# A two-layer transformer kernel on one core: adds moved from TensorE to VectorE, attention weights spread by two DMAs, and the order of the steps rearranged

## Chip, cores and metric

The kernel runs on one core of a Trainium2 chip. The metric is the device time of one execution in microseconds (us); medians are of three to seven runs. All runs quoted here were fast (none is over 0.5% above the fastest run of its kernel). A ratio is the mean time of one kernel's fast runs over that of the other's of the same rounds, so it is not quite the ratio of the medians that stand beside it. The profile is one execution, and its span is 1.7 to 1.8 us shorter than the time of that same run.

Names: PE is TensorE, DVE is VectorE, ACT is ScalarE, POOL is GpSimd; SP issues the weight loads. "oT" is the attention output that the output projection Wo reads; "abc" holds the attention weights, spread over 128 partitions; "a" is the softmax result from which abc is made; "tmp" is the DVE instruction that frees an accumulator of the second feed-forward GEMM.

## The reference, cut to what matters

```python
# B=1, S=2048, D=1024, F=3584, 32 heads of 32; windows of 8 positions, dilation 2
def _A_ref(x, wqkv, wo):                 # local attention
    q, k, v = ...                        # x @ wqkv
    kg, vg = k[..., idx_c, :], v[..., idx_c, :]      # 8 earlier positions: s, s-2, ... s-14
    logits = einsum("bhsd,bhswd->bhsw", q, kg) * scale     # masked at the start of the sequence
    o = einsum("bhsw,bhswd->bhsd", softmax(logits), vg)
    return o @ wo
def _B_ref(x, w1, b1, w2, b2):           # feed-forward
    return gelu(x @ w1 + b1) @ w2 + b2
x = x + _A_ref(layernorm(x), A_wqkv, A_wo);  x = x + _B_ref(layernorm(x), B_w1, B_b1, B_w2, B_b2)
x = x + _A_ref(layernorm(x), A_wqkv, A_wo);  x = x + _B_ref(layernorm(x), B_w1, B_b1, B_w2, B_b2)
```

## The kernel before

The sequence is cut into four groups of 512 tokens. Two layers times four groups make eight steps, n = 0 to 7. A step is: q, k, v projections (24 chunks of 8 matmuls), attention, Wo (8 chunks), first GEMM (28 units of 8 matmuls), second GEMM (32 units of 7). PE works in the program's order: its timeline of one middle step of the kernel before shows Wo (394.73 us), the projections (407.90) with the head sum among them (458.37), the first GEMM and then the second (498.64). DVE work of the next step is laid beside PE work of this one by hand: `stage(gen, count, sides)` runs a generator of PE units and calls the side functions at the given units.

The attention of one step has four parts. DVE makes q·k products for 8 chunks; a matmul with a 0/1 matrix sums them over a head into PSUM (L, a "head sum", one group of 8 matmuls). `attend` is the softmax. `spread` copies each head's weights to four partitions, by writing them to DRAM and reading them back, or by matmul. `av` multiplies with v and sums (4.3 us of DVE per chunk, eight chunks).

```python
def spread(n, on_pe=False):
    ...
    if on_pe:                                     # steps 0, 1 and 7
        ... 8 matmuls with selbc and 8 ACT copies; return
    a_d = dram.tile([H, W, T], BF16, name="a_d")
    for tb in range(NTT):                         # 4 DMAs out
        pool.dma_start(a_d[:, :, tb * P:(tb + 1) * P], a[tb * H:(tb + 1) * H, :, :])
    for j in range(HP):                           # 4 DMAs in
        pool.dma_start(abc[j::HP, :, :], a_d[:, :, :])

def gen_ffn2(n):
    for dh in range(2):
        pss = [acc_tile() for _ in range(NTT)]    # 4 of the 6 accumulators
        for kq in range(4):
            ... load one weight tile
            for tt in range(NTT):
                ... 7 matmuls
                if kq == 3:                       # the accumulator is freed by DVE
                    vec.tensor_tensor(out=tmp[:], in0=pss[tt][:], in1=b2bc[...], op=ALU.add)
                    vec.tensor_tensor(out=xs, in0=tmp[:], in1=xs, op=ALU.add)
                yield

# the schedule of most steps
for n in range(2, N - 1):
    stage(gen_wo(n))
    stage(gen_qkv(n + 1))
    last = n + 2 == N
    stage(gen_ffn1(n), sides=at(4, attend, n + 1) + at(9 if last else 4, spread, n + 1, last) + each(av, n + 1, 9, 2))
    ...
```

## Time and profile before

| | before |
|---|---|
| time, median of 3 | 1281.39 us (1280.09 to 1281.58) |
| span of the profile | 1278.2 us |
| PE busy / DVE busy | 1252.9 / 808.3 us |
| GEMM matmuls | 5632, 215.9 ns apart when nothing interrupts |

First part of the page of the kernel before: busy time, share of the span, instructions.

```profile
PE 1252.9 (98%) x5861; PEld 630.7 (49%) x5910; DVE 808.3 (63%) x843; ACT 322.4 (25%) x502; POOL 85.0 (7%) x217
```

The waits view of PE before: what PE waited for, us in total, times, longest.

```profile
PE L L115 <- DVE big L93: 3.7, 6, 2.5
PE acc L115 <- DMA wt<-in_A_wo_dram: 3.3, 1, 3.3
PE acc L115 <- ACT abc L93: 2.7, 2, 2.4
PE acc L115 <- DVE x_91 L93: 2.3, 1, 2.3
...
```

PE is the bottleneck, and it hardly waits. 5632 x 215.9 ns is 1216 us, so all else that PE does or waits for is 62 us: that is all that a change of schedule can win.

The DMA part of the page (count, KB each, median us from issue to landing):

```profile
abc<-a_d POOLq DMA_DIRECT2D x20, 256.0 KB, 4.2
a_d<-a POOLq DMA_DIRECT2D x20, 64.0 KB, 2.1
```

The four DMAs out were issued in 2.35 us and had landed 2.18 us later. From the end of a to the first v product took 10.8 us here.

### The profile page before, as it was taken

To read this page: it belongs to the slowest core of one execution; us is meant where nothing else is said; L and a number is where in the kernel's file an instruction comes from. 1 tells how busy PE (TensorE), PEld (TensorE's weight loads), DVE (VectorE), ACT (ScalarE), POOL (GpSimd) and SP (SyncE) were. 2 spreads that over 40 slices of the span, in tenths; PEclk is the share of its full clock that TensorE was granted. 3 is DMA by queue.
4 is the path that set the end of the run, shared out by engine and by line. 5 is a ranking of instruction groups with operands and counts; after the bars stand their busy time and mean duration, and the time that the engine had idled before them with its cause. 6 is when DMAs were issued, how large, how long until landed. Compare 5 with 4: busy or idle time off the path is not lost.

```text
span 1278.2 us, 14116 instructions
## 1 busy us (share of the span) xinstructions
PE 1252.9 (98%) x5861; PEld 630.7 (49%) x5910; DVE 808.3 (63%) x843; ACT 322.4 (25%) x502; POOL 85.0 (7%) x217
## 2 busy tenths in 40 slices
PE   9989899999999999999999999999999999999998
PEld 5546454444445644456444554446544464444443
DVE  4877489977317769279583696837875557942003
ACT  4353243102300342013510235002440035300410
POOL 4010000020000020000200002000030000000000
PEclk9989999999999999999999999999999999999999
DMA  8663364385546465555556655565566564466441
GB/s 280 190 164 132 132 174 151 108 238 178 160 153 181 147 202 160 177 162 176 185 161 187 187 164 178 164 203 156 185 186 187 177 196 132 146 175 202 140 144 51
DMA packets 216352, 216.42 MB, mean 169 GB/s; under 512 B 67808, under 2 KB 186592, under 8 KB 213600
## 3 DMA queue, kind: packets, MB, share of 16 engines
q1 hardware_dynamic: 214528, 208.69, 54.4%
q0 software_dynamic: 1760, 6.83, 1.7%
q8 instruction: 46, 0.75, 0.2%
q14 instruction: 18, 0.15, 0.0%
HBM read 194.26 MB, written 5.51 MB: 156 GB/s over the span
## 4 chain that ended last, share of the span: by engine, by line
PE 75%; DVE 18%; issue 2%; ACT 2%; DMA 2%; SPq 0%; POOL 0%; DVEq 0%; ACTq 0%; POOLq 0%
PE acc L115 74%; DVE big L93 17%; DMA x_91<-in_A_x_dram 1%; PE L L115 1%; ACT abc L93 1%; ACT xn L93 0%; DVE z L93 0%; DVE stats L93 0%; DMA wt<-in_A_wo_dram 0%; DMA xnT<-xn 0%; SPq L93 0%; ACT kT L93 0%; ACT qT L93 0%; DVE oT L93 0%; DVE a L93 0%
## 5 line engine op out<-in xcount | busy, mean ns | idle before, releaser
L115 PE MATMUL acc<-xnT,wt 128*128 128x512 bf16 x3328 | 728.3, 381 | 3.0 <-ACT abc L93 2.4
L115 PEld LDWEIGHTS <-wt 128*128 128x128 bf16 x3328 | 395.3, 119 | 334.3 <-issue 17.4
L115 PE MATMUL acc<-wt,hT 128*128 128x512 bf16 x1752 | 386.5, 379 | 2.1
L115 PEld LDWEIGHTS <-hT 128*128 128x128 bf16 x1792 | 175.2, 98 | 211.7 <-issue 0.4
L93 ACT ACTIVATE hT<-acc,b1T 128x512 bf16<-128x512 f32 x224 | 152.7, 687 | 266.4 <-PE acc L115 265.7
L93 DVE TENSOR_TENSOR tmp<-acc,b2bc 128x512 f32<-128x512 f32 x64 | 44.2, 690 | 271.8 <-PE acc L115 269.0
L93 DVE TENSOR_TENSOR big<-big 128x1024 bf16<-128x1024 bf16 (+2 forms) x170 | 209.9, 1279 | 1.2
L93 DVE TENSOR_TENSOR big<-qT,kT 128x4096 bf16<-128x4096 bf16 x64 | 143.6, 2286 | 63.7 <-ACT kT L93 54.4
L93 DVE TENSOR_TENSOR big<-abc,vT 128x4096 bf16<-128x4096 bf16 x64 | 143.5, 2282 | 22.3 <-ACT abc L93 15.3
L93 ACT CAST qT<-acc 128x512 bf16<-128x512 f32 x64 | 37.0, 585 | 373.7 <-PE acc L115 373.7
L115 PE MATMUL acc<-wt,oT 128*128 128x512 bf16 x503 | 115.0, 387 | 6.2 <-DMA wt<-in_A_wo_dram 3.3
L115 PEld LDWEIGHTS <-oT 128*128 128x128 bf16 x512 | 50.8, 99 | 69.0 <-issue 11.2
L93 POOL TENSOR_TENSOR rstd<-mv,eps_t 128x1 f32<-128x1 f32 x64 | 12.8, 201 | 792.0 <-DVE mv L93 791.1
L93 ACT CAST kT<-acc 128x512 bf16<-128x512 f32 x64 | 37.3, 587 | 78.0 <-PE acc L115 78.0
L93 ACT CAST vT<-acc 128x512 bf16<-128x512 f32 x64 | 37.6, 588 | 76.2 <-PE acc L115 76.2
L93 POOL TENSOR_TENSOR rstd<-rstd,mhalf 128x1 f32<-128x1 f32 x64 | 38.4, 601 | 5.0
L93 POOL DMA_DIRECT2D a_d<-a x20 | 11.8, 615 | 235.6 <-DVE a L93 235.6
L93 ACT ACT_TABLE_LOAD x14 | 18.0, 1283 | 35.1 <-PE acc L115 34.1
L93 DVE TENSOR_REDUCE z<-e 128x128 f32<-128x1024 f32 x8 | 15.3, 1915 | 13.8 <-ACT e L93 13.8
L93 DVE TENSOR_TENSOR oT<-big 128x512 bf16<-128x512 bf16 x64 | 24.0, 413 | 0.0
L93 ACT ACTIVATE e<-e 128x1024 f32<-128x1024 f32 x8 | 8.5, 1058 | 34.8 <-DVE e L93 34.7
L115 PE MATMUL L<-big,smat 128*32 128x512 bf16 x176 | 13.2, 384 | 3.7 <-DVE big L93 3.7
(116 smaller groups left out, 336.8 us busy)
## 6 DMA issues: line engine op xcount, KB each, us to landing
wt<-in_B_w_dram SPq DMA_DIRECT2D x56, 1024.0 KB, 5.5
wt<-in_B_w_dram SPq DMA_DIRECT2D x64, 896.0 KB, 4.9
wt<-in_A_wqkv_dram SPq DMA_DIRECT2D x48, 1024.0 KB, 5.5
wt<-in_A_wo_dram SPq DMA_DIRECT2D x16, 1024.0 KB, 5.0
abc<-a_d POOLq DMA_DIRECT2D x20, 256.0 KB, 4.2
a_d<-a POOLq DMA_DIRECT2D x20, 64.0 KB, 2.1
xnT<-xn SPq DMA_TRANSPOSE x60, 5.0
x_87<-in_A_x_dram SPq DMA_DIRECT2D x1, 256.0 KB, 2.7
```

The costliest lines, as they stand in the source:

```text
L93: inst = f(*args, **kwargs)
L115: return pe(nc.tensor.matmul(*args, **kwargs))
```

## The change

Its intent is to take work from PE and to remove PE's few waits:

- In steps 0 and 1 DVE adds the chunk products, so two head sums per step are left of eight (12 more DVE adds of 2.29 us).
- All spreads go by DMA (none by matmul), and by two DMAs rather than eight.
- The layernorms of groups 1 and 2 come before the first products and are normalized by DVE.
- The v weights of some steps are loaded later. Wo of steps 1 and 7 stands after 6 units of the second GEMM, not 4; products of steps 1, 2 and 7 are split around other work; attention of the middle steps starts at unit 7, not 4; that of step 2 at unit 12 of the first GEMM of step 1.

```diff
-    def head_sum(n, prod, last):
+    def head_sum(n, last=True):
...
-        if s["on_pe"]:
-            if len(tree) > 2:
-                head_sum(n, tree.pop(0), False)
-        elif c % 2 == 1:
-            for _ in range(min(2, len(tree) - 1)):
+        if c % 2 == 1:
+            for _ in range(1 if c % (NCH // s["parts"]) == 1 else 2):
                 b = tree.pop()
                 vec.tensor_tensor(out=tree[-1][:], in0=tree[-1][:], in1=b[:], op=ALU.add)
...
-        for tb in range(NTT):
-            pool.dma_start(a_d[:, :, tb * P:(tb + 1) * P], a[tb * H:(tb + 1) * H, :, :])
-        for j in range(HP):
-            pool.dma_start(abc[j::HP, :, :], a_d[:, :, :])
+        pool.dma_start(a_d[:].rearrange("h w (b t) -> b h w t", b=NTT), a[:])
+        src = a_d[:]
+        pool.dma_start(abc[:], bass.AP(tensor=src.tensor, offset=src.offset, ap=[[W * T, H], [0, HP], [1, W * T]]))
...
+        stage(gen_qkv(0, 2), sides=at(0, ln_a, 1) + at(2, load_x, 2) + at(4, ln_a, 2, early) + ... + at(18, head_sum, 0, False))
+        stage(q1, sides=at(3, attend, 0) + at(3, spread, 0) + each(new_prod, 1, 8, 1, 0, 4) + each(av, 0, 12, 1))
...
-    stage(f2, 4)
+    stage(f2, 6)
     stage(gen_wo(1))
...
+    stage(gen_ffn1(1), sides=at(0, hold) + each(new_prod, 2, 0, 1, 4, 8) + at(12, attend, 2) + at(12, spread, 2) + each(av, 2, 13, 2))
...
-        stage(gen_ffn1(n), sides=at(4, attend, n + 1) + at(9 if last else 4, spread, n + 1, last) + each(av, n + 1, 9, 2))
+        stage(gen_ffn1(n), sides=at(7, attend, n + 1) + at(7, spread, n + 1) + each(av, n + 1, 9, 2))
...
+    q = gen_qkv(n + 1, defer=True, v_late=True)          # n = 6
+    stage(q, 16, sides=each(new_prod, n + 1, 8, 1, 0, 4))
+    stage(gen_wo(n))
+    stage(q, sides=each(new_prod, n + 1, 0, 1, 4, 8))
+    stage(gen_ffn1(n), sides=at(3, attend, n + 1) + at(3, spread, n + 1) + each(av, n + 1, 4, 2))
+    f2 = gen_ffn2(n)
+    stage(f2, 6)
+    stage(gen_wo(n + 1))
+    stage(f2)
```

The DMA out: its DRAM side has dimensions 4 (token blocks) x 32 (heads) x 8 x 128, so the outermost one counts 4.

More of the change, by code (lines that the diff above doesn't have):

```diff
@@ L75 @@
     smp = ctx.enter_context(tc.tile_pool(name="smp", bufs=1))
-    iop = ctx.enter_context(tc.tile_pool(name="iop", bufs=2))
+    iop = ctx.enter_context(tc.tile_pool(name="iop", bufs=1))
     psum = ctx.enter_context(tc.tile_pool(name="psum", bufs=1, space=PSUM))
@@ L135 @@
     smat = const.tile([P, H], BF16, name="smat")
-    selbc = const.tile([P, P], BF16, name="selbc")
     maskrow = const.tile([1, W, 16], BF16, name="maskrow")
@@ L156, in build_constants @@
         pool.memset(onesrow[:], 1.0)
-        pool.memset(selbc[:], 1.0)
-        for tb in range(NTT):
-            sb = selbc[tb * H:(tb + 1) * H, :]
-            pool.affine_select(out=sb, in_=sb, pattern=[[1, P]], compare_op=ALU.is_ge, fill=0.0, base=0, channel_multiplier=-HP)
-            pool.affine_select(out=sb, in_=sb, pattern=[[-1, P]], compare_op=ALU.is_ge, fill=0.0, base=HP - 1, channel_multiplier=HP)
     def load_bias():
@@ L179, in ln_stats, with ln_norm, ln_tile @@
         return mv, rstd
-    def ln_norm(t, mv, rstd, on_act=False):
-        xn = lnp.tile([P, D], BF16, name="xn")
-        if on_act:
-            nmr = lnp.tile([P, 1], F32, name="nmr")
-            pool.tensor_tensor(out=nmr[:], in0=mv[:, 0:1], in1=rstd[:], op=ALU.mult)
-            pool.tensor_scalar(out=nmr[:], in0=nmr[:], scalar1=-1.0, scalar2=None, op0=ALU.mult)
-            act.activation(xn[:], x[t][:], ACT.Identity, bias=nmr[:], scale=rstd[:])
-        else:
-            vec.tensor_scalar(out=xn[:], in0=x[t][:], scalar1=mv[:, 0:1], scalar2=rstd[:], op0=ALU.subtract, op1=ALU.mult)
+    def ln_norm(t, mv, rstd):
+        xn = lnp.tile([P, D], BF16, name="xn", bufs=3)
+        vec.tensor_scalar(out=xn[:], in0=x[t][:], scalar1=mv[:, 0:1], scalar2=rstd[:], op0=ALU.subtract, op1=ALU.mult)
         return xn
-    def ln_tile(t, tt, xnT, on_act=False):
+    def ln_tile(t, tt, xnT):
         mv, rstd = ln_stats(t)
-        xn = ln_norm(t, mv, rstd, on_act)
+        xn = ln_norm(t, mv, rstd)
         sp.dma_start_transpose(xnT[:, tt, :, :], xn[:].rearrange("s (k p) -> s k p", p=P))
@@ L211, in ln_first, with new_xnT @@
         vec.on = False
-    def new_xnT():
-        return xnp.tile([P, NTT, KD, P], BF16, name="xnT")
+    def new_xnT(pool=None):
+        return (pool or xnp).tile([P, NTT, KD, P], BF16, name="xnT")
     def win(t_ap):
@@ L238, in qkv_chunk @@
         return ps
-    def head_sum(n, prod, last):
-        first = "L" not in st[n]
-        if first:
+    def head_sum(n, last=True):
+        if "L" not in st[n]:
             st[n]["L"] = psum.tile([P, W, P], F32, name="L", bufs=1)
+            start = True
+        else:
+            start = False
         L = st[n]["L"]
+        first = n % NG == 0
+        prod = st[n]["prods"].pop(0)
         for wh in range(2):
@@ L247, in head_sum @@
                 mm(L[tb * H:(tb + 1) * H, wh * 4:(wh + 1) * 4, :], lhsT=smat[:],
-                   rhs=prod[:, wh * 4:(wh + 1) * 4, tb * P:(tb + 1) * P],
-                   start=first, stop=last, skip_group_check=True, tile_position=(0, tb * H))
+                   rhs=prod[:, wh * 4:(wh + 1) * 4, tb * P:(tb + 1) * P], start=start,
+                   stop=last and not (first and tb == 0), skip_group_check=True, tile_position=(0, tb * H))
+        if first and last:
+            for w in range(W - 1):
+                mm(L[0:H, w, 0:HALO], lhsT=onesrow[:], rhs=maskrow[0:1, w, 0:HALO], start=False, stop=True,
+                   skip_group_check=True, tile_position=(0, 0))
     def new_prod(n, c):
@@ L257, in new_prod, with gen_qkv @@
         tree.append(prod)
-        if s["on_pe"]:
-            if len(tree) > 2:
-                head_sum(n, tree.pop(0), False)
-        elif c % 2 == 1:
-            for _ in range(min(2, len(tree) - 1)):
+        if c % 2 == 1:
+            for _ in range(1 if c % (NCH // s["parts"]) == 1 else 2):
                 b = tree.pop()
                 vec.tensor_tensor(out=tree[-1][:], in0=tree[-1][:], in1=b[:], op=ALU.add)
-    def gen_qkv(n, sum_on_pe=False, defer=False, qk_pool=None):
+    def gen_qkv(n, parts=1, defer=False, qk_pool=None, v_late=False):
         g = n % NG
@@ L269, in gen_qkv @@
         s = st[n]
-        s["on_pe"] = sum_on_pe
+        s["parts"] = parts
         s["prods"] = []
@@ L282, in gen_qkv @@
             yield
-        wv = load_qkv(2)
+        if not v_late:
+            wv = load_qkv(2)
         kT = qk_pool.tile([P, NCH, HALO + T], BF16, name="kT")
@@ L296, in gen_qkv @@
         s["vT"] = vT
+        if v_late:
+            wv = load_qkv(2)
         act.copy(vT[:, :, 0:HALO], (zhalo if g == 0 else vhalo)[:])
@@ L307, in attend @@
         s = st[n]
-        while s["prods"]:
-            head_sum(n, s["prods"].pop(0), not s["prods"])
+        head_sum(n)
         L = s.pop("L")
-        if n % NG == 0:
-            for w in range(W - 1):
-                mm(L[0:H, w, 0:HALO], lhsT=onesrow[:], rhs=maskrow[0:1, w, 0:HALO], start=False, stop=True,
-                   skip_group_check=True, tile_position=(0, 0))
         mx = smp.tile([P, P], F32, name="mx")
@@ L325, in attend, with spread @@
         s["a"] = a
-    def spread(n, on_pe=False):
+    def spread(n):
         s = st[n]
@@ L333, in spread @@
         s["oT"] = attp.tile([P, NCH, T], BF16, name="oT")
-        if on_pe:
-            for wh in range(2):
-                for tb in range(NTT):
-                    ps = acc_tile()
-                    mm(ps[:], lhsT=selbc[tb * H:(tb + 1) * H, :], rhs=a[tb * H:(tb + 1) * H, wh * 4:(wh + 1) * 4, :],
-                       start=True, stop=True, tile_position=(tb * H, 0))
-                    act.copy(abc[:, wh * 4:(wh + 1) * 4, tb * P:(tb + 1) * P], ps[:].rearrange("p (w t) -> p w t", w=4))
-            return
         a_d = dram.tile([H, W, T], BF16, name="a_d")
-        for tb in range(NTT):
-            pool.dma_start(a_d[:, :, tb * P:(tb + 1) * P], a[tb * H:(tb + 1) * H, :, :])
-        for j in range(HP):
-            pool.dma_start(abc[j::HP, :, :], a_d[:, :, :])
+        pool.dma_start(a_d[:].rearrange("h w (b t) -> b h w t", b=NTT), a[:])
+        src = a_d[:]
+        pool.dma_start(abc[:], bass.AP(tensor=src.tensor, offset=src.offset, ap=[[W * T, H], [0, HP], [1, W * T]]))
     def av(n, c):
@@ L419, in warm_up, with ln_a @@
             mm(ps[:], lhsT=warm[:], rhs=warm[:].unsqueeze(1).to_broadcast([P, NTT, P]), start=True, stop=True)
-    def ln_a(n, on_act=False):
-        xa[n] = new_xnT()
+    def ln_a(n, pool=None):
+        xa[n] = new_xnT(pool)
         for tt in range(NTT):
-            ln_tile((n % NG) * NTT + tt, tt, xa[n], on_act)
+            ln_tile((n % NG) * NTT + tt, tt, xa[n])
     def stage(gen, count=None, sides=()):
@@ L445, in each, with hold @@
         return [(int(u0 + du * (c - c0)), lambda c=c: f(n, c)) for c in range(c0, c1)]
+    def hold():
+        vec.bar = True
     pool.on = True
@@ L450 @@
     build_constants()
-    def ln2():
-        vec.bar = True
-        ln_a(2, True)
-    stage(gen_qkv(0, sum_on_pe=True), sides=at(0, load_x, 1) + at(2, ln_a, 1, True) + at(12, load_x, 2) + at(16, load_x, 3)
-          + at(20, load_bias) + at(18, attend, 0))
-    with tc.tile_pool(name="early", bufs=1) as early:
-        q1 = gen_qkv(1, sum_on_pe=True, defer=True, qk_pool=early)
-        stage(q1, sides=at(0, ln2) + at(1, spread, 0, True) + each(av, 0, 2, 1))
-        q2 = gen_qkv(2, defer=True)
-        stage(q2, 16, sides=each(new_prod, 1, 2, 1.5))
-        stage(gen_wo(0), sides=at(1, attend, 1))
-        stage(q2, sides=at(2, spread, 1, True) + each(av, 1, 3, 1))
+    with tc.tile_pool(name="early", bufs=1) as early:
+        load_x(1)
+        stage(gen_qkv(0, 2), sides=at(0, ln_a, 1) + at(2, load_x, 2) + at(4, ln_a, 2, early) + at(12, load_x, 3) + at(18, load_bias)
+              + at(18, head_sum, 0, False))
+        q1 = gen_qkv(1, 2, defer=True, qk_pool=early)
+        stage(q1, sides=at(3, attend, 0) + at(3, spread, 0) + each(new_prod, 1, 8, 1, 0, 4) + each(av, 0, 12, 1))
+        q2 = gen_qkv(2, defer=True, v_late=True)
+        stage(q2, 16)
+        stage(gen_wo(0))
+        stage(q2, sides=each(new_prod, 1, 0, 1, 4, 8) + at(2, head_sum, 1, False))
@@ L463 @@
     hpool = ctx.enter_context(tc.tile_pool(name="hpool", bufs=1))
-    stage(gen_ffn1(0), sides=each(new_prod, 2, 20, 1))
+    stage(gen_ffn1(0), sides=at(0, attend, 1) + at(0, spread, 1) + at(0, hold) + each(new_prod, 2, 0, 1, 0, 4) + each(av, 1, 4, 2))
     f2 = gen_ffn2(0)
-    stage(f2, 4)
+    stage(f2, 6)
     stage(gen_wo(1))
-    stage(f2, sides=at(2, attend, 2) + at(2, spread, 2))
-    stage(gen_ffn1(1), sides=each(av, 2, 1, 2))
+    stage(f2)
+    stage(gen_ffn1(1), sides=at(0, hold) + each(new_prod, 2, 0, 1, 4, 8) + at(12, attend, 2) + at(12, spread, 2) + each(av, 2, 13, 2))
@@ L470 @@
     stage(gen_ffn2(1), sides=at(2, ln_a, 3))
-    for n in range(2, N - 1):
+    for n in range(2, N - 2):
         stage(gen_wo(n))
         stage(gen_qkv(n + 1))
-        last = n + 2 == N
-        stage(gen_ffn1(n), sides=at(4, attend, n + 1) + at(9 if last else 4, spread, n + 1, last) + each(av, n + 1, 9, 2))
-        f2 = gen_ffn2(n)
-        if not last:
-            stage(f2, sides=at(2, ln_a, n + 2))
-        else:
-            stage(f2, 4)
-            stage(gen_wo(n + 1))
-            stage(f2)
+        stage(gen_ffn1(n), sides=at(7, attend, n + 1) + at(7, spread, n + 1) + each(av, n + 1, 9, 2))
+        stage(gen_ffn2(n), sides=at(2, ln_a, n + 2))
@@ L483 @@
+    n = N - 2
+    q = gen_qkv(n + 1, defer=True, v_late=True)
[6 more added lines that the diff above has]
+    stage(gen_wo(n + 1))
+    stage(f2)
     stage(gen_ffn1(N - 1))
```

## The prediction

> **What bounds the kernel now.** TensorE. The page's first part has PE busy 1252.9 of 1278.2 us (DVE 63%). The ScalarE timeline shows PSUM evictions of consecutive projection chunks 1.727 us apart, so one 128x512 matmul costs 215.9 ns[...]. The 5632 GEMM matmuls are then 1216 us. The other 62 us, from the PE timeline: 13.8 before the first projection, 4.5 after the last matmul, 22 head-sum groups, three spreads by matmul, and waits.
>
> **Removed.**
> - Head sums: steps 0 and 1 drop from 8 groups of 8 matmuls to 2 each. With a group between chunks, evictions stand 2.43 us apart, so a group costs 0.70 us: 12 x 0.70 = 8.4 us.
> - Spreads by matmul (steps 0, 1, 7): about 6.5 us of PE time with its waits at 66.9-73.5, 2.2 at 171.3, 2.5 at 1080: 11 us.
> - PE waits listed by the waits view: 2.5 (first head sum), 3.3 (first Wo weights; V weights now come after them), 2.3 (Wo of step 1 behind products), five of 0.24.
> - Cold matmuls after those waits: 18 after 73.5 us take 0.35 us each, 12 after 150.3 take 0.37, 7 after 242.4 take 0.4: 2.4 + 1.8 + 1.3 us.[...]
>
> All on the critical path, as PE is: about 36 us.
>
> **Added or moved.** DVE gets 12 more 128x4096 adds (2.29 us each, 27 us) and 8 layernorm normalizations (0.5 us each) that ScalarE had. DVE has room overall, but the first 220 us are nearly balanced between DVE and PE:
> - Start: one more statistic enters the first chain: +0.6 us.
> - Step 0: two layernorms end near 32 us, first partial sum near 48, PE asks at 47: 0-3 us wait. Value products (8 x 4.28 us) end near 124, before Wo asks at 127.
> - Step 1: attention starts about 158, then four products with three adds (15.9 us), then 34.2 us of value products, ending about 217; PE reaches Wo about 213: wait 4 us, cold matmuls 2 us.
> - Step 7: products are split around Wo of step 6; a product and an add precede its last normalization on DVE, so the first GEMM waits about 2.5 us. Softmax ends near 17 us after that GEMM's start, the two DMAs take about 11 us (10.9 with eight), value products 34.2: Wo waits 4 us, cold 2 us.
>
> **Sum.** -36 +0.6 +1.5 +6 +8.5 = about -20 us. Predicted 1260 us, 80% between 1252 and 1270. Faster by over 2%: 0.22; within 2%: 0.75; slower: 0.03.
>
> **What would show it.** PE timeline: L groups 10 instead of 22, no selbc matmuls, first projection at 14-15 us; second GEMM of step 1 ending about 24 us earlier than 394 us, most of the gain; steps 2 to 5 unchanged within 0.5 us each (152.9 us period); PE waits for oT at Wo of steps 1 and 7, 3-5 us each.
>
> **What would make it wrong.** Layernorm of group 2 held up by transposes queued behind 4 MB of weights; the single a-to-DRAM DMA, whose outer dimension is 4, [...]taking 5-10 us longer, which adds to step 7's wait[...].

(Passages that no trace or run of this case shows are cut at the marks. No term of the sum is among them; it came to about -20 us, and so to 1260. The 2 us of cold matmuls at each of two Wo are estimates, from the 2.4, 1.8 and 1.3 us found in the trace of before; the 11 us of the two DMAs is an estimate from the 10.9 measured with eight.)

## More of the kernel before

The trace also records the granted clock, the share of its full clock at which TensorE was let run: in the traces of before and after it is 1.00 or 0.50. GEMM matmuls there begin 216 ns apart at 1.00 and 427 ns apart at 0.50 (medians).

The spread by DMA, in the POOL timeline of one middle step (start, us, instruction, in brackets the idle time before it):

```profile
468.39 2.35 POOL L93 DMA_DIRECT2D a_d<-a  x4 [56.11 <-DVE a L93]
472.92 2.08 POOL L93 DMA_DIRECT2D abc<-a_d  x4 [2.18 <-DMA a_d<-a]
```

## The result

The changed kernel takes 1293.03 us (median of 4, 1292.6 to 1293.46) against 1280.74 us: ratio 1.0098, 95% interval 1.008 to 1.0115. It is 1% slower. The prediction was 1260, with a range of 1252 to 1270.

The same views after. First part of the page:

```profile
PE 1241.0 (96%) x5740; PEld 628.5 (49%) x5790; DVE 842.8 (65%) x863; ACT 305.1 (24%) x472; POOL 81.9 (6%) x168
```

PE lost 12 us of work as intended, yet the span grew by 12.6 us. The waits view says what came in:

```profile
PE acc L115 <- DVE oT L93: 17.4, 3, 7.5
PE acc L115 <- DVE tmp L93: 14.0, 4, 11.1
PE L L115 <- DVE big L93: 5.4, 2, 4.7
PE acc L115 <- ACT vT L93: 1.3, 1, 1.3
...
```

Two kinds of wait that did not exist before now cost 31.4 us. Both name DVE, and DVE has 35 us more to do: it would be easy to stop here and call DVE overloaded. The POOL timeline of the same middle step, and the DMA part of the page, point elsewhere:

```profile
471.04 2.07 POOL L93 DMA_DIRECT2D a_d<-a  x1 [61.14 <-DVE a L93]
482.85 0.58 POOL L93 DMA_DIRECT2D abc<-a_d  x1 [9.73 <-DMA a_d<-a]
```

```profile
abc<-a_d POOLq DMA_DIRECT2D x8, 1024.0 KB, 5.9
a_d<-a POOLq DMA_DIRECT2D x8, 256.0 KB, 11.5
```

The one DMA out moves the same 256 KB as the four before it. POOL waited 9.73 us for it after issuing it, where it had waited 2.18 us for four. From the end of a to the first v product the middle steps took 17 to 18 us and step 7 took 21.2 us, where before the DMA spreads took 10.5 to 11.9. POOL's layernorm work (rstd) also stood behind its wait: DVE's waits for rstd add up to 90.4 us here and to 47.1 before. In the steps looked at, abc still landed after that work was done, so abc is what the v products waited for.

Where PE stood still, in its timeline (start, us, instruction, in brackets the wait before it):

```profile
226.93 1.46 PE L115 MATMUL acc<-wt,oT 128*128 128x512 bf16 x3 [5.60 <-DVE oT L93]
...
368.83 23.02 PE L115 MATMUL acc<-wt,hT 128*128 128x512 bf16 x96 [11.05 <-DVE tmp L93]
...
524.31 21.32 PE L115 MATMUL acc<-wt,hT 128*128 128x512 bf16 x96 [1.01 <-DVE tmp L93]
...
1126.68 1.03 PE L115 MATMUL acc<-wt,oT 128*128 128x512 bf16 x2 [4.32 <-DVE oT L93]
1135.23 1.46 PE L115 MATMUL acc<-wt,oT 128*128 128x512 bf16 x3 [7.52 <-DVE oT L93]
```

The waits at 226.93, 1126.68 and 1135.23 are Wo of steps 1 and 7, standing before oT. The one at 368.83 lies inside the second GEMM of step 1: its second half needs an accumulator that DVE frees only after all v products of step 2. In the DVE timeline the first of these v products wait for abc, and the tmp behind them begins at 368.09:

```profile
333.43 4.50 DVE L93 TENSOR_TENSOR big<-abc,vT 128x4096 bf16<-128x4096 bf16 x2 [2.32 <-DMA abc<-a_d]
```

The stretch after it shows a second cost. 96 recorded matmuls took 23.02 us there, and 21.32 us after the short wait at 524.31: the granted clock had dropped to 0.50 from 362.1 to 372.3 us.

The chain of waits between 1060 and 1150 us shows the mechanism in one piece (start, us, what; each piece was released by the one above):

```profile
1080.47 12.50 DMA a_d<-a
1092.97 0.30 issue
1093.27 7.92 DMA abc<-a_d
...
1101.22 7.97 DVE big L93 x6
...
1134.84 0.35 DVE oT L93
...
1135.23 1.46 PE acc L115 x3
```

DVE did not fall behind here. It stood idle until 1101, waiting for abc (21.2 us, the longest of these waits in the waits view of DVE below), and then needed its 34 us as always.

```profile
DVE big L93 <- DMA abc<-a_d: 31.7, 7, 21.2
```

### The profile page after: what moved, and what is told of

The parts are those of the page before. It is cut to its first block, busy times and chain, and to the rows that moved or that the text cites. A ratio compares the mean times of both kernels' runs of the same rounds, so it can differ in the third digit from the quotient of the medians.

```text
span 1290.8 us, 13810 instructions
## 1 busy us (share of the span) xinstructions
PE 1241.0 (96%) x5740; PEld 628.5 (49%) x5790; DVE 842.8 (65%) x863; ACT 305.1 (24%) x472; POOL 81.9 (6%) x168
## 5 line engine op out<-in xcount | busy, mean ns | idle before, releaser
L93 DVE TENSOR_TENSOR big<-big 128x1024 bf16<-128x1024 bf16 (+2 forms) x182 | 237.6, 1349 | 1.5
L115 PE MATMUL acc<-wt,oT 128*128 128x512 bf16 x500 | 117.0, 391 | 18.4 <-DVE oT L93 17.4
L93 POOL TENSOR_TENSOR rstd<-mv,eps_t 128x1 f32<-128x1 f32 x64 | 16.8, 262 | 592.9 <-DVE mv L93 592.9
L93 POOL DMA_DIRECT2D a_d<-a x8 | 16.6, 2074 | 375.0 <-DVE a L93 375.0
L93 DVE TENSOR_REDUCE mx<-L 128x128 f32<-128x1024 f32 x8 | 9.8, 1225 | 33.0 <-PE L L115 33.0
## 6 DMA issues: line engine op xcount, KB each, us to landing
a_d<-a POOLq DMA_DIRECT2D x8, 256.0 KB, 11.5
```

Of the source, the lines that this page charges most:

```text
L93: inst = f(*args, **kwargs)
L115: return pe(nc.tensor.matmul(*args, **kwargs))
```

## The experiments

Theory A: the single DMA out is slow because few of its packets are under way at once (in the trace of the changed kernel at most 5 in steps 1 to 7, and 16 for the four DMAs before); this delays the v products of the middle steps by 6 to 8 us, more than the schedule has to spare, and PE pays at Wo and at tmp. Theory B: DVE has too much work. A third question was whether the single DMA in is slow as well. Eleven kernels were run, each timed against the kernel before in three rounds.

### e1_eight_dmas: the old DMAs back in the changed kernel

```diff
-        pool.dma_start(a_d[:].rearrange("h w (b t) -> b h w t", b=NTT), a[:])
-        src = a_d[:]
-        pool.dma_start(abc[:], bass.AP(...))
+        for tb in range(NTT):
+            pool.dma_start(a_d[:, :, tb * P:(tb + 1) * P], a[tb * H:(tb + 1) * H, :, :])
+        for j in range(HP):
+            pool.dma_start(abc[j::HP, :, :], a_d[:, :, :])
```

> The changed kernel with the eight DMAs per spread of before put back (four out, four in), nothing else. Theory A (one DMA out to DRAM [...]takes 8 to 9 us instead of 2, delays the value products by about 9 us in each step, and this surfaces as the waits of PE for oT and tmp): a to abc back to about 11 us; wait before the second GEMM of step 1 from 11.05 to about 2 us, the 1 us waits of steps 2, 3 and 5 gone, Wo of step 7 from 11.8 to about 3 us, Wo of step 1 from 5.6 to about 2; time about 1268 us, ratio to before 0.99. Theory B (DVE has too much work: 12 adds and 8 normalizations, 31 us): waits and time unchanged within 3 us, about 1292.

Measured: 1261.83 us, ratio 0.9855 (0.9838 to 0.9871), correct. This one edit is worth 31 us. The DMA out lands after 2.2 us again. The PE timeline, at the same places as above:

```profile
222.73 12.81 PE L115 MATMUL acc<-wt,oT 128*128 128x512 bf16 x56 [1.75 <-DVE oT L93]
...
353.23 21.32 PE L115 MATMUL acc<-wt,hT 128*128 128x512 bf16 x96 [2.22 <-DVE tmp L93]
...
1105.73 12.81 PE L115 MATMUL acc<-wt,oT 128*128 128x512 bf16 x56 [3.69 <-DVE oT L93]
```

The waits of 5.60, 11.05 and 11.84 (4.32 + 7.52) us became 1.75, 2.22 and 3.69, and those of 1 us in the later steps are gone. The gain was somewhat larger than expected. Laid out by where the two PE timelines part, the 31.9 us between the spans (1290.8 and 1258.9) fall so: 6.4 us around Wo of step 1, 10.5 in the second GEMM of step 1, 3.5 in steps 2 to 5, 11.1 around Wo of step 7, and 0.4 before. Of the 31.9, the listed waits for oT and tmp are 23.8 (31.4 against 7.6). Most of the rest is the clock: PE worked 17.7 us at half clock in the changed kernel and 3.4 in e1, which by our estimate cost about 9 and 2 us (half of each, as a matmul takes 427 ns at half clock and 216 at full).

### e7_no_adds_01: 27 us of DVE work taken away instead

```diff
                 b = tree.pop()
+                if s["parts"] == 2:
+                    continue
                 vec.tensor_tensor(out=tree[-1][:], in0=tree[-1][:], in1=b[:], op=ALU.add)
```

> The changed kernel without the 12 adds of steps 0 and 1 on DVE (27 us of DVE work taken away; the head sums see half of the products, so the result is wrong on purpose). Theory A: early waits shrink (first head sum 4.7 us, Wo of step 1 partly), gain 5 to 12 us, but the waits of steps 1 (second GEMM), 2, 3, 5 and 7 stay: time about 1281 to 1288. Theory B (DVE overloaded by them): most of the loss returns, time about 1262 to 1270.

Measured: 1290.82 us, ratio 1.0078 (1.0063 to 1.0093). Its output is wrong, which doesn't matter for the time. The wait for the first head sum is gone, but the others stand:

```profile
222.45 1.46 PE L115 MATMUL acc<-wt,oT 128*128 128x512 bf16 x3 [5.75 <-DVE oT L93]
...
363.71 22.71 PE L115 MATMUL acc<-wt,hT 128*128 128x512 bf16 x96 [11.04 <-DVE tmp L93]
...
1132.43 1.46 PE L115 MATMUL acc<-wt,oT 128*128 128x512 bf16 x3 [7.70 <-DVE oT L93]
```

Theory B falls: without all the added adds the kernel gains 2 us, which is hardly more than the noise. (The 8 layernorm normalizations of about 0.5 us each stayed, but e1 is fast with both.) That is less than theory A expected, too, for the early gain of 5 us was partly eaten by other waits (2.0 us for weights, more at tmp).

### e5_one_out_outer128: still one DMA, same bytes and pieces, other outer dimension

```diff
-        pool.dma_start(a_d[:].rearrange("h w (b t) -> b h w t", b=NTT), a[:])
+        dst = a_d[:]
+        pool.dma_start(bass.AP(tensor=dst.tensor, offset=dst.offset, ap=[[P, P], [P * P, W], [1, P]]), a[:])
```

The order in DRAM is wrong, so the result is. No run has a single DMA with this DRAM order and a larger outer dimension. The question is whether the time follows the outer dimension (theory A1) or the use of one DMA (A2).

> The changed kernel, but its one DMA out writes the same 256 KB in the same 256-byte pieces with an outer dimension of 128 instead of 4 (the order in DRAM is then wrong, so the result is wrong on purpose; nothing else changes). Theory A1[...]: packets of 4096 bytes run up to 16 at once instead of 4 to 5, out DMA 2 to 3 us, time about 1268 us as with eight DMAs. Theory A2 (one big DMA is slow as such, for example by its 2 us issue): packets still few at once, time about 1290.

Measured: 1259.56 us, ratio 0.9833 (0.9818 to 0.9847). One DMA was not slow as such: this one landed after 3.3 us. The DRAM order that e5 gave up is not to blame either: the four DMAs of e1 write in that order and landed after 2.2 us. The line of e5 in the DMA part of the page, to be read against 11.5 above:

```profile
a_d<-a POOLq DMA_DIRECT2D x8, 256.0 KB, 3.3
```

The trace records every packet. Counted from these records, for the 64 packets of 4096 bytes of one DMA out (in the kernel before and in e1, of the four together), seven of the eight steps:

```
                      packets under way at most   from first to last packet
before                16                          2.0 to 2.2 us
changed                5                          7.8 to 9.2 us
eight DMAs (e1)       16                          1.6 to 2.5 us
outer 128 (e5)        16 to 20                    1.0 to 2.2 us
```

(Step 0 of the last three is left out, and the kernel before has five DMA spreads. In step 0 the changed kernel took 4.4 us, with at most 6 packets under way; e1 and e5 took 2.4. The same records show what else was moving: in steps 1 to 7 of the changed kernel 0.8 to 1.0 MB of other transfers, mostly weights, ran beside the DMA out, and in step 0 only 0.06 MB. So 4.4 us is nearer to what so few packets at once cost alone. That the weight loads stretched it to 7.8 to 9.2 us is the author's guess; no run tests it.) So the number of packets under way went with the outer dimension of the DRAM side: with 4 it was 5 at most and 2.7 to 3.4 on average in steps 1 to 7, with 128 it was 16 to 20 at most, for the same bytes in the same pieces. Why 4 keeps so few under way the trace does not show.

### e3_four_out_one_in and e4_one_out_four_in: which of the two DMAs

The first takes from the eight only the four DMAs out, the second only the four in.

```diff
# e3
-        pool.dma_start(a_d[:].rearrange("h w (b t) -> b h w t", b=NTT), a[:])
+        for tb in range(NTT):
+            pool.dma_start(a_d[:, :, tb * P:(tb + 1) * P], a[tb * H:(tb + 1) * H, :, :])
# e4
-        src = a_d[:]
-        pool.dma_start(abc[:], bass.AP(tensor=src.tensor, offset=src.offset, ap=[[W * T, H], [0, HP], [1, W * T]]))
+        for j in range(HP):
+            pool.dma_start(abc[j::HP, :, :], a_d[:, :, :])
```

> The changed kernel with four DMAs out (one per token block, outer dimension 32) but still one DMA in. Theory A: the loss comes from the out DMA alone, so this is as fast as with all eight, 1258 to 1263 us, ratio 0.982 to 0.987; a to abc 10 to 12 us. If the single DMA in carries part of the loss: between 1265 and 1285.

> The mirror of it: one DMA out with outer dimension 4, four DMAs in. Theory A: the loss stays, 1290 to 1295 us, ratio 1.007 to 1.011; 4096-byte packets 4 to 5 at once for 8 to 9 us. If the single DMA in carries part of it: below 1285.

Measured: e3 1262.79 us, ratio 0.9856 (0.9827 to 0.9885): as fast as with all eight. The single DMA in is blameless. In the traces of e3, e4 and e5 DVE and ACT run the same instructions in the same order as in the changed kernel, so nothing but the DMAs differs. (In e1 DVE's order differs a little in step 1.) e4 took 1307.64 us, ratio 1.0205 (1.0176 to 1.0233), 15 us above what was expected. With four DMAs in, the time from a to the first v product was 20 to 21 us in the middle steps, some 2 to 3 us more than the 17 to 18 of the changed kernel; issuing four takes POOL 2.08 us instead of 0.58. There was no slack left to hide this, as the second GEMMs of steps 2 to 4 show:

```profile
527.98 22.94 PE L115 MATMUL acc<-wt,hT 128*128 128x512 bf16 x98 [3.73 <-DVE tmp L93]
685.57 22.65 PE L115 MATMUL acc<-wt,hT 128*128 128x512 bf16 x98 [2.95 <-DVE tmp L93]
842.35 22.77 PE L115 MATMUL acc<-wt,hT 128*128 128x512 bf16 x98 [2.68 <-DVE tmp L93]
```

Where the changed kernel waited 0 to 1.1 us per step, this one waits 2.7 to 3.7 in the three lines shown (3.96 in step 5), and the matmuls behind each wait are 1.3 to 1.6 us slower in sum than 21.32 (2.6 in step 5). So 2 to 3 us of delay cost about 4 us in each of these steps.

### e2_before_two_dmas: the two DMAs alone, in the kernel before

The edit is the DMA part of the change in the five DMA spreads of before.

> The kernel before with only its five DMA spreads turned into two DMAs each. Theory A: a to abc grows from 11 to about 20 us, but its attention starts at unit 4 of the first GEMM, value products would end about 522 us in the step whose second GEMM starts at 499 and needs an accumulator freed at about 525, so PE hides it: time within 2 us of before, ratio 1.000 to 1.003. If the DMA alone costs time wherever it stands: ratio about 1.01.

Measured: 1284.84 us, ratio 1.003 (1.0012 to 1.0048), correct, at the upper end of what was expected. From a to the first v product takes 17.4 to 18.6 us here too, but PE pays once, and only 3.70 us, in the first GEMM of step 1, behind v products of step 2:

```profile
307.32 46.73 PE L115 MATMUL acc<-xnT,wt 128*128 128x512 bf16 x208 [3.70 <-DVE tmp L93]
```

Even this is not the DMA's alone: the build of e2 put DVE's instructions in another order there. Four chunks of v products stand before this tmp, where in the kernel before two products did. So the same slow DMA costs about 4 us in the old schedule and 31 in the new one. The old one starts attention three units (5 us) earlier in the middle steps and spreads by matmul where it is tight, in step 7. The new one had spent this slack.

### e9_wo_after_12: the slow DMA kept, Wo later

```diff
     f2 = gen_ffn2(0)
-    stage(f2, 6)
+    stage(f2, 12)
...
     f2 = gen_ffn2(n)
-    stage(f2, 6)
+    stage(f2, 12)
```

> The changed kernel with its slow DMA kept, but Wo of steps 1 and 7 after 12 units of the second GEMM instead of 6 (9.1 us more of GEMM work in front of it). If the waits at Wo are lateness of the value products and nothing else: step 1 waits 0 instead of 5.6, step 7 about 3 instead of 11.8, the 11 us before the second GEMM of step 1 stays; time 1274 to 1279 us, ratio 0.995 to 0.999.

Measured: 1274.54 us, ratio 0.9954 (0.9939 to 0.9969), correct.

```profile
360.89 23.62 PE L115 MATMUL acc<-wt,hT 128*128 128x512 bf16 x98 [10.40 <-DVE tmp L93]
...
1128.42 12.81 PE L115 MATMUL acc<-wt,oT 128*128 128x512 bf16 x58 [2.35 <-DVE oT L93]
```

The wait at Wo of step 1 is gone, that of step 7 is 2.35 us, and that at tmp stays: as expected. The lateness can also be paid for by putting other PE work in front of it.

### v1_four_one_all, v2_one_four_all, e10_e1_headsum_later, v3_attend_later: towards a faster kernel

With the DMA mended, the profile of e1 still listed 5.1 us at the first head sum, 1.75 and 3.69 at Wo, and 2.22 at tmp. Version v1 takes the four DMAs out and one in of e3, and moves PE work in front of these waits:

```diff
-... + at(18, head_sum, 0, False))
+... + at(21, head_sum, 0, False))
-    stage(f2, 6)                     # steps 1 and 7
+    stage(f2, 12)
-... at(12, attend, 2) + at(12, spread, 2) + each(av, 2, 13, 2)
+... at(10, attend, 2) + at(10, spread, 2) + each(av, 2, 11, 2)
```

Version v2 has the same schedule, with one contiguous DMA out and four in:

```diff
+        a_d = dram.tile([P, W, P], BF16, name="a_d")     # as a lies: 128 rows of 2 KB
+        pool.dma_start(a_d[:], a[:])
+        for tb in range(NTT):
+            src = a_d[tb * H:(tb + 1) * H]
+            pool.dma_start(abc[:, tb], bass.AP(tensor=src.tensor, offset=src.offset, ap=[[W * P, H], [0, HP], [1, W * P]]))
# abc is [P, NTT, W, P]; av reads it through rearrange("p b w t -> p w b t")
```

> A version meant to beat both: four DMAs out and one in, the first head sum of step 0 three chunks later in PE order, Wo of steps 1 and 7 after 12 units of the second GEMM instead of 6 or 4, attention of step 2 two units earlier. From the waits left in the run with eight DMAs (5.1 first head sum, 1.8 and 3.7 at Wo, 2.2 before the second GEMM of step 1, and 2 to 3 of cold matmuls): 1247 to 1252 us, ratio 0.974 to 0.978.

> The same schedule with one contiguous DMA out (128 rows of 2 KB) and four in (one per token block, 256 KB each), the spread weights kept by token block and read through a rearranged view. Result correct. If the out DMA of one instruction is fast once its outer dimension is 128: a to abc 8 to 10 us and time equal to the four-and-one version within 2 us; if the four-dimensional view slows the products on DVE (2.28 us each before), later by that.

Measured: v1 1251.90 us, ratio 0.9774 (0.9751 to 0.9797); v2 1253.78 us, ratio 0.9781 (0.9753 to 0.981); both correct. They cannot be told apart. From a to the first v product v2 took 12 to 15 us in the middle steps and not the 8 to 10 expected: its DMA out was issued in 0.59 us and POOL waited 2.9 to 5.1 us more for it (v1: 2.35 and 2.0 to 3.1 for its four), but its four DMAs in took POOL 2.17 us to issue, against 0.57 for the one of v1. How much of the 12 to 15 us each part explains was not worked out. The waits of v1 at Wo and tmp are gone, but a wait of 2.6 us at the second head sum of step 0 and one of 1.4 us for weights had appeared, so two more runs looked at that corner: e10 is e1 with only `at(21, head_sum, 0, False)`; v3 is v1 with

```diff
-        stage(q1, sides=at(3, attend, 0) + at(3, spread, 0) + ...
+        stage(q1, sides=at(5, attend, 0) + at(5, spread, 0) + ...
```

> The run with eight DMAs, plus the first head sum of step 0 three chunks later in PE order. The 5.1 us wait there goes away, but the next head sum of step 0 waits for DVE about 2.6 us and a weight load about 1.4 us, as in the version with all four edits: gain over the run with eight DMAs 1 to 3 us, 1259 to 1261 us, ratio 0.983 to 0.985.

> The version with all four edits, plus attention of step 0 two chunks later (unit 5 instead of 3), so that its second head sum does not wait 2.6 us for DVE. If PE order is all that this wait is about: 1249 to 1251 us, ratio 0.975 to 0.977; if DVE work moves later by as much and Wo of step 0 then waits: no gain.

Measured: e10 1263.34 us, ratio 0.9864 (0.9847 to 0.988), not told apart from e1 (0.9855), where 1 to 3 us of gain were expected. They were run at other times. Removing the first wait alone gained nothing measurable: DVE's chain of products handed most of it to the next head sum (2.86 us) and to a weight load (1.09 us). The comparison can't show the remaining 1 us: in the profile of e10 the clock also dropped after the waits at tmp (2.20 us) and at Wo of step 7 (3.86), which it had not after those of e1 (2.22 and 3.69), and the matmuls behind them took 3.3 us longer. v3 took 1247.60 us, ratio 0.9743 (0.9728 to 0.9757), correct, and a little better than the 1249 to 1251 expected: 33 us and 2.6% faster than before, 3.5% faster than the changed kernel by their medians. The waits of PE that are left in v3:

```profile
PE L L115 <- DVE big L93: 2.8, 3, 1.4
PE acc L115 <- ACT vT L93: 1.2, 1, 1.2
PE acc L196 <- DVE xn L93: 1.2, 2, 0.8
...
```

All of v3's DVE work is that of the changed kernel (840.8 us in 863 instructions, against 842.8 in 863), and its clock never dropped between 5 and 1243 us (mean of the span: 0.999).

## Why the prediction was wrong, point by point

- **What bounds the kernel, and what is removed: right.** The PE timeline shows 10 head sums, no spread by matmul, and the first projection at 14.18 us (said: 14 to 15).
- **The step that failed is the term "the two DMAs take about 11 us (10.9 with eight)".** It measured 21.2 us in step 7 and 17 to 20 in steps 1 to 6. The duration of eight DMAs was carried over to two of another shape. The risk was named (a single DMA "whose outer dimension is 4", "taking 5-10 us longer"; by the medians from issue to landing it took 9.4 us longer, 11.5 against 2.1), but it stayed among the risks and did not enter the sum.
- **"which adds to step 7's wait" was too narrow.** The DMA stands in every step. Step 7 paid 11.1 us, the second GEMM of step 1 paid 10.5, Wo of step 1 6.4, and steps 2 to 5 together 3.5. For the middle steps the prediction ("unchanged within 0.5 us each") looked only at whether oT is ready for the next Wo, which it is; it did not ask when the tmp instructions run, which DVE's order puts behind the v products and which PE needs in the middle of the second GEMM.
- **With the term put right, the sum holds.** With eight DMAs the changed kernel took 1261.83 us, against 1260 predicted. The period of a middle step there is 152.6 to 152.9 us (said 152.9). The closeness is in part luck, for its terms were off by up to 4 us either way: the first head sum waited longer and tmp, which was not in the sum, waited 2.2 us, while the waits at Wo and the slow matmuls after them cost less.
- **Smaller terms.** First head sum of step 0: 4.7 us in the changed kernel and 5.1 with eight DMAs, predicted 0 to 3; the second layernorm ended at 35.9 us rather than 32, as its inputs were loaded behind transposes. Waits at Wo of steps 1 and 7 with the DMA mended: 1.75 and 3.69, predicted 4 and 4, and no slow matmuls after them, where 2 us each were reckoned. That, too, was luck of the clock: in e10, waits of nearly the same length at tmp (2.20 us, e1 2.22) and at Wo of step 7 (3.86, e1 3.69) were followed by slow ones.
- **"Second GEMM of step 1 ending about 24 us earlier than 394 us"** was the right thing to look at: it ended at 391.7, so the loss was visible a third of the way in; with eight DMAs, at 374.4.

What stays open: why an outer dimension of 4 leaves so few packets under way, how much of the slow DMA out is due to that alone and how much to the weight loads beside it, and why the four DMAs in of e4 end 2 to 3 us later, of which the issue explains 1.5. Why the clock sometimes drops after a wait of a given length and sometimes does not was not shown (the cases measured are below).

## What to carry to other kernels

Fewer DMAs were not faster here: one of 256 KB took 11.5 us from issue to landing where four of 64 KB took 2.1. Before merging several, look at the outermost dimension on the DRAM side (here 4, against 32 in the four DMAs and 128 in e5, which took 3.3 us), and read the time from issue to landing and not the issue count. A wait that names a compute engine need not mean that this engine is busy: PE's 7.52 us at Wo of step 7 named DVE, which had itself stood idle for 21.2 us. Follow the chain one step further up, and test it by taking the engine's work away. The same slow DMAs cost about 4 us in the old schedule (e2) and 31 in the new one (e1), where the slack before them was spent, so merging work and tightening the schedule should be tried apart before together.

## What else the traces show of the DMAs and the clock

- From issue to landing (median) the DMA out of 256 KB took 3.3 us with outer dimension 128 (e5) and 11.5 us with 4 (changed kernel).
- With outer dimension 4 its packets took 4.4 us beside 0.06 MB of other transfers and 7.8 to 9.2 beside 0.8 to 1.0 MB. With 128 they mostly took 1.3 us, beside at most 0.05 MB.
- POOL's issue time went with the shape: one DMA of 256 KB took 2.07 us to issue with outer dimension 4 (changed kernel), 0.95 with 128 (e5; both in 256-byte pieces), and 0.59 as 128 contiguous rows (v2).
- The length of a wait alone did not tell whether the clock would drop. After a wait of 2.08 us in e5 the granted clock was 0.57 between 354 and 358 us and 96 matmuls took 23.00 us; after one of 3.28 us in e3 it stayed at 1.00 and 98 took 21.32. e1 and e10 differ in the same way (above).
- From 3.8 us, where its record begins (3.7 in the changed kernel), to the last matmul, the clock's stretches at half clock lasted 6.83, 3.41, 3.41 and 3.41 us in the kernel before, and 3.41, 6.83, 10.24 and 13.65 us in the changed kernel. What sets these lengths was not shown.

The stretches after the two waits of e5 and e3, in the view of busy time by stretches (stretch, its length, busy us and count of PE, PEld, DVE, ACT and POOL, granted clock, DMA share, GB/s), first e5, then e3:

```profile
354.00:358.00 4.00, 4.00 (x12) 1.45 (x12) 3.62 (x6) 0.00 (x0) 0.00 (x0) 0.57 0.87 135
```

```profile
353.70:363.00 9.30, 9.23 (x43) 4.20 (x43) 4.86 (x8) 0.00 (x0) 0.00 (x0) 1.00 0.51 143
```
